# Shorter warm-up, halved first transposes, a halved last product and other places for the last x tiles, in a one-core block kernel with a planned order

## The chip, the cores and the metric

One NeuronCore of a Trainium2 chip runs the whole kernel as one program. The time is the device time of one execution in microseconds (us). The kernel before has a median of 604.91 us over three runs (604.63, 604.91 and 607.84). One further execution was profiled: it took 605.64 us, and its trace spans 603.5 us from the first to the last instruction. The 2.14 us between the two lie around the span.

Engines are called by their short names: PE multiplies matrices (PEld is its weight load), DVE and ACT work on vectors, POOL is GpSimd, and SP issues the DMAs.

## The reference

The input x has 2048 tokens of width 512. What has to be computed, cut to its core:

```python
xn = layernorm(x)                                   # no gain, no bias
q, k, v = split(xn @ wqkv)                          # 32 heads of width 16
phi = lambda t: where(t > 0, t + 1, exp(t)) + 1e-6
kv = einsum("bhsd,bhse->bhde", phi(k), v);  z = phi(k).sum(tokens)
s = (phi(q) @ kv) / (phi(q) . z + 1e-6)  @ wo       # linear attention
g = silu((gelu(xn @ w_gate) * (xn @ w_up)) @ w_down)  # F = 1792
return x + s * g
```

## The kernel before, in words

**Arithmetic.** Every large product is made in float32 accuracy from three single passes: each operand is split into a high part (cast by ACT) and a low part (what is left, subtracted by DVE or POOL), and the passes are high x high, high x low and low x high (`split`, `three`). The FFN products and most of the q and k products are moreover made by a Strassen scheme with seven block products instead of eight, so that DVE, ACT and POOL form sums of blocks and add up results while PE multiplies.

**Stages.** First the tokens are read, normalised (`ln`, L639 to L648), transposed by PE (`transp`, L696, a bank of PSUM named `pt`) and split into `Xh` and `Xl` (`split_x`). The first two pairs of token tiles get plain products for k and q (`plain`, keys "K" and "Q"); later pairs get Strassen products (keys "A"). The sums over tokens for the attention are collected in four banks (`gps`, keys "G"). Then come the two halves of the FFN (keys "F" for gate and up, "E" for down), and the attention's last product (keys "S", tiles `sps`), whose four column chunks are worked in the order 2, 3, 0, 1 (`CHUNKS`). For each of the last chunks `out_tile` multiplies the accumulated and silu'd FFN result (`acc` or a tile `g` read back from DRAM) by the product, adds the matching tile of x (read again, `sxr`) and stores it to `out_yT`.

**The front.** PE begins with idle products of a matrix of ones: `WARM[0]` = 14 of them, each of which is two matmul instructions, in bank 0 (`warm`, L561). Behind the first tile's four transposes stand `WARM[1]` = 3 more. The first tile's four transposes are one piece of work for the planner; its split is made in two halves (each 128x256), which both follow that one piece.

**The end.** The very last product, chunk 1 and n = 3, is 12 matmuls of 512 columns into one bank. Its multiplication, addition and store are made in two column halves, both of which follow the whole product. The last tiles of x are loaded into places shared with `g` and other FFN tiles (`SPOTS`), and a load waits until the tile that was there has been stored.

**What sets the order.** Nothing is issued in the order of the code. Each piece of work is an `Op` with an engine, an assumed cost, and what it depends on. `Plan.order` lays the pieces out with these costs, and then re-deals them: each entry of the table `KEPT` names a stretch of assumed time and a seed, from which pieces there get another due time (`altered`), and the whole order is planned again. The result fixes the order on each engine: PE may take a piece up to 6 us of assumed time (`AHEAD`) out of its listed turn. On the chip each engine then goes through its own list strictly in order and waits where an operand, a bank or a place isn't ready; SP's list of DMAs is in order too. So a piece that waits holds back all that stands behind it on its engine.

Of the kernel before, what the change touches and what calls it, by code (L numbers as in the profile page):

```python
# [16 lines left out]
EPS_LN = 1e-5  # L17
EPS = 1e-6
KEPT = [
    (85, 100, [10000006]),  # L20
    (70, 85, [10000048]),
    (-1, 12, [10000061]),
    (40, 55, [10000175]),
    (135, 200, [10000200]),
    (25, 40, [10000230]),
    (40, 55, [10000342]),
    (85, 100, [10000376]),
    (40, 55, [10000415, 10000462]),
    (500, 560, [10000471]),
    (-1, 12, [10000515]),  # L30
    (500, 560, [10000523, 10000590, 10000640]),
    (115, 135, [10000649]),
    (500, 560, [10000723]),
    (115, 135, [10000785]),
    (500, 560, [10000819, 10000833]),
    (340, 420, [10000924]),
    (115, 135, [10000994]),
    (-1, 12, [10001161, 10001223, 10001300]),
    (270, 340, [10001313, 10001357]),
    (-1, 12, [10001377]),  # L40
    (500, 560, [10001410]),
    (-1, 12, [10001492]),
    (40, 55, [10001818]),
    (-1, 12, [10001854]),
    (500, 560, [10001973]),
    (340, 420, [10002732]),
    (135, 200, [10006848]),
    (85, 100, [10010611]),
    (270, 340, [10010753]),
    (40, 55, [10010839]),  # L50
    (340, 420, [10010858]),
    (500, 560, [10010942, 10011053]),
    (40, 55, [10011765]),
    (135, 200, [10011937]),
    (-1, 12, [1010000092]),
    (340, 420, [1010000637, 1010002072]),
    (25, 40, [1010003933]),
    (500, 560, [1010016325, 1010018040]),
    (70, 85, [1010018047, 1010018667, 1010018893, 1010020523]),
    (55, 70, [1010020607]),  # L60
    (85, 100, [1010021997]),
    (100, 115, [1010030646]),
    (115, 135, [1010032131]),
    (100, 115, [1010033698]),
    (500, 560, [1010034750, 1010034866]),
    (135, 200, [1010038225]),
]

TABLES = {"exp": "exp", "gelu": "gelu", "silu": "silu"}
# [326 lines left out]
def kernel(  # L396
# [66 lines left out]
    def bank(i, name, shape=(P, D)):  # L463
        return tile_in("ps", i, list(shape), F32, name)
# [95 lines left out]
        for _ in range(n):  # L560
            nc.tensor.matmul(o, w, w, start=True, stop=True)  # L561
# [127 lines left out]
    def transp(n, i):  # L689
        t = tokens[n][i]  # L690

        pt = bank(3 + 2 * n + i if 0 < 2 * n + i < 2 * CL else 1, f"pt{t}", (P, KT, P))

        def run(o, a, b):
            for k in range(KT):
                nc.tensor.transpose(o[:, k, :], a[:, k * P:(k + 1) * P], b)  # L696
# [25 lines left out]
    def split_x(n, i):  # L722
        if i == 0 and n == 0:
            for s in range(2):
                split(xrows("h", s, s + 1, [0]), xrows("l", s, s + 1, [0]), pts[0, 0][:, 2 * s:2 * s + 2], 2 * P, "Xa")
# [166 lines left out]
    pe_keys.append(("T", 0, 0))  # L892
    for m, (n, i) in enumerate(tiles):
        plain_keys("K", n, i)
        if m + 1 < len(tiles):
# [381 lines left out]
    def attn(c, M, place):  # L1277
# [29 lines left out]
    def out_tile(c, n, ps):  # L1307
# [9 lines left out]
            parts = 2 if (c, n) == (CHUNKS[-1], KT - 1) else 1  # L1317
            w = NC // parts
            for m in range(parts):
                cs = slice(m * w, (m + 1) * w)  # L1320
                o = columns(g, m, parts)
                if ps.psum:
                    do("DVE", dve(w), lambda o, i: nc.vector.tensor_mul(o, o, i), o, ps[:, cs])
                else:
                    tt("DVE", "mul", o, o, ps[:, cs], w)
# [9 lines left out]
    def sums(c):  # L1335
        return [("S", c, n) for n in range(KT)]

    def between(p, wait, s):
# [89 lines left out]
```

## Time and profile before

| what | value |
|---|---|
| median of the runs shown | 604.91 us |
| the profiled execution's own time | 605.64 us |
| its span | 603.5 us |
| PE busy | 594.2 us (98% of the span) |
| DVE, ACT, POOL busy | 517.0, 347.1 and 243.0 us |
| moved by DMA | 137.09 MB, 227 GB/s over the span |

The profile shows, for each engine, when an instruction ran, how long it was busy, and what ended the idle time ahead of it. PE's matmuls are pipelined: a row says how long they were in flight together, and a 512-column matmul that takes 390 ns follows the last one after some 227 ns. A row of the timeline has the start, the length, the engine, the line of the code, the operation, the tile written and the tiles read, and the number of instructions merged in the row. A row of the windows has the two ends, the length, and then for each engine its busy time and the count of instructions.

### The profile page before, as it was taken

Reading aid. Unit: us, or ns where it says so; the run is one execution under the profiler, and the core shown is the slowest. Engines: PE = TensorE matmul, PEld = TensorE weight load, DVE = VectorE, ACT = ScalarE, POOL = GpSimd, SP = SyncE. Lnnn points to the kernel's source line nnn. Section 1 sums busy time; section 2 is a strip of 40 time slices with the busy share of each in tenths; the row PEclk is TensorE's granted clock in tenths of the full one; section 3 lists DMA queues with packets and bytes.
Section 4 is the critical chain, followed back from the end, with each engine's and each line's share of the span. In section 5 each row is a group of like instructions: output and inputs, shape, how many; then the busy total and the mean of one; then the engine's idle time right before and its main releaser. Section 6 shows DMA issues by size and latency. Waiting matters only on the chain.

```text
span 603.5 us, 7883 instructions
## 1 busy us (share of the span) xinstructions
PE 594.2 (98%) x2636; PEld 483.4 (80%) x2636; DVE 517.0 (86%) x819; ACT 347.1 (58%) x627; POOL 243.0 (40%) x237
## 2 busy tenths in 40 slices
PE   9999999999999999999999999999999999999996
PEld 7887877788878888888888777788888888886885
DVE  6999998787689899999899766668899898987995
ACT  6687888787576655655344566655353444445530
POOL 4456757757535372615053830522222130325000
PEclk9999999999999999999999999999999999999998
DMA  7259954779863344667964999744555665568577
GB/s 243 70 154 273 292 187 137 220 212 352 349 232 129 134 175 174 223 225 270 364 213 153 364 394 351 299 164 153 191 193 191 204 215 190 194 202 295 195 252 259
DMA packets 73384, 137.09 MB, mean 227 GB/s; under 512 B 4352, under 2 KB 43264, under 8 KB 69248
## 3 DMA queue, kind: packets, MB, share of 16 engines
q1 hardware_dynamic: 73344, 136.59, 64.8%
q8 instruction: 21, 0.34, 0.2%
q14 instruction: 19, 0.16, 0.1%
HBM read 85.72 MB, written 50.86 MB: 226 GB/s over the span
## 4 chain that ended last, share of the span: by engine, by line
PE 87%; DVE 6%; DMA 4%; ACT 1%; issue 1%; POOL 0%; DVEq 0%; ACTq 0%; POOLq 0%
PE FX L531 24%; PE FZ L531 12%; PE dX L531 11%; PE gps L531 7%; PE FY L531 6%; PE dZ L531 5%; PE X L531 5%; PE dY L531 3%; PE Z L531 2%; PE k L531 2%; PE q L531 2%; PE sps L531 2%; DMA sxr<-in_A_xT 2%; PE Y L531 1%; DMA pql<-t_d 1%
## 5 line engine op out<-in xcount | busy, mean ns | idle before, releaser
L531 PE MATMUL FX<-Xh,w 128*128 128x512 f32 x448 | 135.2, 391 | 0.0
L531 PEld LDWEIGHTS FX<-Xh,w 128*128 128x128 f32 x448 | 83.9, 188 | 18.3 <-ACT fu L498 0.6
L1194 POOL TENSOR_TENSOR h<-h,g 128x512 f32<-128x512 f32 x28 | 41.3, 1475 | 99.5 <-DVE h L504 95.5
L531 PE MATMUL FZ<-Xh,w 128*128 128x512 f32 x224 | 69.8, 393 | 0.0
L531 PE MATMUL FX<-Xl,w 128*128 128x512 f32 x224 | 68.9, 390 | 0.1
L1154 DVE TENSOR_TENSOR acc<-acc,dX 128x512 f32<-128x512 f32 x76 | 51.8, 681 | 19.4 <-PE dX L531 18.9
L498 ACT CAST hfh<-sums 128x512 fp32r<-128x512 f32 x56 | 34.5, 622 | 48.9 <-DVE sums L504 48.4
L498 ACT COPY fu<-FX 128x512 f32<-128x512 f32 x56 | 32.9, 587 | 42.2 <-PE FX L531 40.6
L504 POOL TENSOR_TENSOR tmp<-raw 128x256 f32<-128x256 f32 x28 | 27.4, 992 | 66.9 <-DVE w L504 35.3
L531 PEld LDWEIGHTS FZ<-Xh,w 128*128 128x128 f32 x224 | 42.0, 188 | 9.9 <-issue 1.0
L531 PEld LDWEIGHTS FX<-Xl,w 128*128 128x128 f32 x224 | 42.0, 188 | 9.2 <-ACT fu L498 0.5
L504 DVE TENSOR_TENSOR hfl<-sums,hfh 128x512 fp32r<-128x512 f32 x56 | 42.5, 764 | 4.2 <-ACT hfh L498 3.3
L531 PE MATMUL dX<-hfl,dh 128*128 128x512 f32 x112 | 43.9, 394 | 1.1 <-DVE acc L1154 0.6
L1007 POOL TENSOR_TENSOR qz<-qz,zq 128x512 f32<-128x512 f32 x16 | 23.4, 1465 | 50.9 <-DMA qz<-q_d 44.5
L531 PE MATMUL dX<-hfh,dl 128*128 128x512 f32 x112 | 43.7, 391 | 0.0
L531 PE MATMUL dX<-hfh,dh 128*128 128x512 f32 x112 | 43.7, 392 | 0.0
L504 POOL TENSOR_TENSOR sums<-draw 128x256 f32<-128x256 f32 x28 | 22.0, 795 | 45.0 <-DMA draw<-in_B_w_down 34.3
L1154 DVE TENSOR_TENSOR acc<-acc,dZ 128x512 f32<-128x512 f32 x52 | 35.5, 683 | 3.9 <-PE dZ L531 3.8
L498 ACT CAST hfh<-h 128x512 fp32r<-128x512 f32 x42 | 26.0, 621 | 15.3 <-POOL h L1194 5.4
L531 PE MATMUL FY<-Xh,w 128*128 128x512 f32 x112 | 34.3, 390 | 0.3 <-ACT FY L498 0.3
L531 PE MATMUL FZ<-Xl,w 128*128 128x512 f32 x112 | 34.3, 390 | 0.0
L504 DVE TENSOR_TENSOR hfl<-h,hfh 128x512 fp32r<-128x512 f32 x42 | 32.8, 781 | 0.0
(197 smaller groups left out, 1490.6 us busy)
## 6 DMA issues: line engine op xcount, KB each, us to landing
w<-w_d SPq DMA_DIRECT2D x17, 1792.0 KB, 7.6
w_d<-w SPq DMA_DIRECT2D x11, 1792.0 KB, 8.0
draw<-in_B_w_down SPq DMA_DIRECT2D x14, 512.0 KB, 6.1
w_d<-we SPq DMA_DIRECT2D x18, 256.0 KB, 3.3
x<-in_A_x SPq DMA_DIRECT2D x16, 256.0 KB, 4.0
q_d<-qp SPq DMA_DIRECT2D x16, 256.0 KB, 2.9
qz<-q_d SPq DMA_DIRECT2D x16, 256.0 KB, 4.5
q<-q_d SPq DMA_DIRECT2D x16, 256.0 KB, 3.3
```

The lines of the kernel that those rows point to most:

```text
L498: do("ACT", act(n, src.psum), lambda o, i: nc.scalar.copy(o, i), dst, src, name=name)
L504: do(eng, c, lambda o, p, q: getattr(e, f"tensor_{op}")(o, p, q), dst, a, b, name=name)
L531: nc.tensor.matmul(o if r is None else o[:, r], a, b, start=first, stop=made == self.passes[r], skip_group_check=self.on or r is not None)
L1007: do("POOL", pool(D), lambda o, z: nc.gpsimd.tensor_mul(o, o, z.unsqueeze(1).to_broadcast([P, KT, P])), rows_of(q), zq, name="u")
L1154: do("DVE", dve(D), lambda o, i: nc.vector.tensor_add(o, o, i), o, ps, name="acc")
L1194: do("POOL", pool(NC), lambda o, i: nc.gpsimd.tensor_mul(o, o, i), h, g, name="h")
```

## The change

It has five parts.

1. **Fewer idle products.** `WARM` goes from 14, 3 to 12, 2, and they use bank 7 instead of bank 0.
2. **The first transposes in two halves.** The first tile's four transposes become two pieces of two, each with half of the bank `pt` as its own resource, so that each half of the split follows its own pair. The remaining idle products stand behind the second pair.
3. **The last product in two column halves.** Chunk 1, n = 3 becomes two sums of 12 matmuls with 256 columns, each in a bank of its own, and its multiplication, addition and store follow half by half.
4. **Places for the last x tiles.** In the last chunk `sxr` goes into `FREED`, the 16 places of the `hfh` and `hfl` tiles, instead of `SPOTS`.
5. **Another deal.** `KEPT` is replaced as a whole, and the assumed cost of a tile's transposes is 0.5 instead of 0.4. This moves instructions on all engines.

The diff, with the table cut to its first line:

```diff
 KEPT = [
-    (85, 100, [10000006]),
+    (-1, 12, [230000004]),
...
-WARM = 14, 3
+WARM = 12, 2
...
-    idle = bank(0, "warm", (P, P))
-    do("PE", 0.427 * 10, warm, idle, ones, key="warm")
+    idle = bank(7, "warm", (P, P))
+    do("PE", 0.427 * 11.5, warm, idle, ones, key="warm")
...
-        pt = bank(3 + 2 * n + i if 0 < 2 * n + i < 2 * CL else 1, f"pt{t}", (P, KT, P))
-        def run(o, a, b):
-            for k in range(KT):
-                nc.tensor.transpose(o[:, k, :], a[:, k * P:(k + 1) * P], b)
-            if n == 0 and i == 0:
-                warm(idle(), ones(), WARM[1])
-        do("PE", 0.4, run, pt, xns[t], ident, key=("T", n, i), name="T", more=(idle,) if n == 0 and i == 0 else ())
+        front = n == 0 and i == 0
+        pt = tile_in("ps", 3 + 2 * n + i if 0 < 2 * n + i < 2 * CL else 1, [P, KT, P], F32, f"pt{t}", 2 if front else 1)
+        for h in range(2 if front else 1):
+            v = pt.part(pt.res[h:h + 1], (slice(None), slice(2 * h, 2 * h + 2))) if front else pt
+            def run(o, a, b, h=h):
+                for k in range(2 if front else KT):
+                    j = 2 * h + k
+                    nc.tensor.transpose(o[:, k, :], a[:, j * P:(j + 1) * P], b)
+                if front and h:
+                    warm(idle(), ones(), WARM[1])
+            do("PE", 0.25 if front else 0.5, run, v, xns[t], ident, key=("T", n, i, h) if front else ("T", n, i), name="T",
+               more=(idle,) if front and h else ())
...
+            if (c, n) == (CHUNKS[-1], KT - 1):
+                halves = []
+                for m in range(2):
+                    cs = slice(m * NC // 2, (m + 1) * NC // 2)
+                    ps = bank(ring("sps", [3, 4, 2, 0, 1]), f"sps{c}{n}{m}", (P, NC // 2))
+                    Sum(ps).add(("S", c, n, m), *three([[v[:, k, rows] for v in M] for k in range(KT)],
+                                                       [[v[:, cs] for v in f] for f in forms_]), name="S", cost=SHORT)
+                    halves.append(ps)
+                out_tile(c, n, halves)
+                continue
...
-            xr = U("g", SPOTS, f"sxr{c}{n}")
+            xr = U(*(("xr", FREED) if c == CHUNKS[-1] else ("g", SPOTS)), f"sxr{c}{n}")
...
+    FREED = [*FHH, *FHL]
```

What this does to the order of the built program, at three places. In each list a row is the line of the code, the operation, what is written and read, and the size; the figures in a name only tell buffers apart.

**First place, the front: SP's DMAs and ACT's casts.** `x` is a tile of tokens, `wk` are the two weight tiles of k (two halves each), `kq` their split. SP before:

```order
L494 DMA x_98<-in_A_x 128x512
L494 DMA wk_119<-in_A_wqkv 128x512 x2
L494 DMA x_124<-in_A_x 128x512
L494 DMA wk_130<-in_A_wqkv 128x512 x2
L494 DMA x_133<-in_A_x 128x512
L494 DMA x_137<-in_A_x 128x512
```

SP in the changed kernel:

```order
L540 DMA x_98<-in_A_x 128x512
L540 DMA x_117<-in_A_x 128x512
L540 DMA wk_123<-in_A_wqkv 128x512 x2
L540 DMA wk_126<-in_A_wqkv 128x512
L540 DMA x_128<-in_A_x 128x512
L540 DMA x_132<-in_A_x 128x512
L540 DMA wk_126<-in_A_wqkv 128x512
```

The second token tile moved from the fourth place to the second, the first weights from second and third to third and fourth, and the last half of the second weights from sixth to eighth. ACT before, from its first weight cast (`pt_156` is the first transposed tile, `pt_196` the second, `xnh` the high part of the tokens):

```order
L498 CAST kq_145<-wk_119 128x512 x2
L498 CAST xnh_166<-xn_152 128x512
L498 CAST Xh_172<-pt_156 128x2x128 x2
L498 CAST kq_145<-wk_130 128x512 x2
L498 CAST xnh_203<-xn_190 128x512
```

ACT in the changed kernel (`pt_159` is the first transposed tile):

```order
L544 CAST kq_154<-wk_123 128x512 x2
L544 CAST Xh_170<-pt_159 128x2x128
L544 CAST kq_154<-wk_126 128x512
L544 CAST xnh_180<-xn_152 128x512
L544 CAST Xh_170<-pt_159 128x2x128
L544 COPY xt_187<-pt_159 128x512
L544 CAST kq_154<-wk_126 128x512
```

The two casts of the first transposed tile no longer stand together: between them stand a cast of the second weights and one of the tokens, and the other half of the second weights comes after both.

**Second place, the first Strassen pair of the tokens: DVE around the split of the last weight form** (`kq` from `wk`, 128x1024). `c` adds a saved result to a bank, `Xl` are low parts of tokens. Before:

```order
L504 TENSOR_TENSOR Xl_183<-T_449,Xh_172 128x4x128 x2
L504 TENSOR_TENSOR Xl_183<-pt_633,Xh_172 128x4x128
L504 TENSOR_TENSOR c_2_664<-u_2_640,Z_575 128x512
L504 TENSOR_TENSOR kq_235<-wk_130,kq_235 128x1024
L504 TENSOR_TENSOR Xl_183<-pt_666,Xh_172 128x2x128
```

In the changed kernel:

```order
L550 TENSOR_TENSOR Xl_178<-T_447,Xh_170 128x4x128
L550 TENSOR_TENSOR Xl_178<-pt_621,Xh_170 128x4x128
L550 TENSOR_TENSOR Xl_178<-T_447,Xh_170 128x4x128
L550 TENSOR_TENSOR kq_297<-wk_126,kq_297 128x1024
L550 TENSOR_TENSOR c_2_668<-u_2_647,Z_601 128x512
```

The split of the weight form now stands ahead of the addition `c` instead of behind it.

**Third place, the end: DVE's last multiplications and additions.** `sps` are the banks of the attention's product, the figure tells them apart. Before:

```order
L504 TENSOR_TENSOR acc_0_4030<-acc_0_4030,sxr_5733 128x512
L504 TENSOR_TENSOR acc_2_3986<-acc_2_3986,sxr_5742 128x512
L1323 TENSOR_TENSOR acc_2_3986<-acc_2_3986,sps_5752 128x512
L504 TENSOR_TENSOR acc_2_3986<-acc_2_3986,sxr_5707 128x512
L1323 TENSOR_TENSOR acc_3_4010<-acc_3_4010,sps_5775 128x512
L504 TENSOR_TENSOR acc_3_4010<-acc_3_4010,sxr_5757 128x512
L1323 TENSOR_TENSOR acc_3_4010<-acc_3_4010,sps_5792 128x256 x2
L504 TENSOR_TENSOR acc_3_4010<-acc_3_4010,sxr_5725 128x256 x2
```

In the changed kernel:

```order
L550 TENSOR_TENSOR acc_0_4027<-acc_0_4027,sxr_5734 128x512
L550 TENSOR_TENSOR acc_2_3983<-acc_2_3983,sxr_5631 128x512
L1386 TENSOR_TENSOR acc_2_3983<-acc_2_3983,sps_5751 128x512
L550 TENSOR_TENSOR acc_2_3983<-acc_2_3983,sxr_5680 128x512
L1386 TENSOR_TENSOR acc_3_4008<-acc_3_4008,sps_5772 128x512
L550 TENSOR_TENSOR acc_3_4008<-acc_3_4008,sxr_5438 128x512
L1384 TENSOR_TENSOR acc_3_4008<-acc_3_4008,sps_5789 128x256
L550 TENSOR_TENSOR acc_3_4008<-acc_3_4008,sxr_5580 128x256
L1384 TENSOR_TENSOR acc_3_4008<-acc_3_4008,sps_5804 128x256
L550 TENSOR_TENSOR acc_3_4008<-acc_3_4008,sxr_5580 128x256
```

The first half is now multiplied and added ahead of the second half's multiplication, and each half has a bank of its own. On SP the last load of an x tile before is `sxr_5757`, with two stores (of `g_5645` and of `acc_0`) ahead of it that stand behind the load of `sxr_5742`; in the changed kernel the last load is `sxr_5734`, and all the remaining stores stand behind it. That load takes the place of `g_5559`, so it waits until that tile is stored.

More of the change, by code (lines that the diff above doesn't have):

```diff
@@ L37 @@
[L37 to L53, printed above, removed]
@@ new lines @@
+    (200, 270, [230000007]),
+    (40, 55, [230000051]),
+    (55, 70, [230000055]),
+    (500, 560, [230000057]),
+    (-1, 12, [230000067]),
+    (270, 340, [230000091]),
+    (500, 560, [230000095]),
+    (115, 135, [230000096]),
+    (500, 560, [230000130]),
+    (115, 135, [230000136]),
+    (70, 85, [230000159]),
+    (270, 340, [230000175]),
+    (500, 560, [230000184]),
+    (-1, 12, [230000189]),
+    (270, 340, [230000192]),
+    (340, 420, [230000237]),
+    (500, 560, [230000265]),
@@ new lines @@
+    (100, 115, [230012249]),
+    (135, 200, [230012251]),
+    (-1, 12, [230012263, 230012268]),
+    (200, 270, [230012291]),
+    (340, 420, [230012323]),
+    (-1, 12, [230012330]),
+    (500, 560, [230012337]),
+    (270, 340, [230012385]),
+    (340, 420, [230012437]),
+    (-1, 12, [230012841]),
+    (115, 135, [230013103]),
+    (500, 560, [230013486]),
+    (270, 340, [230013516]),
+    (85, 100, [230013546]),
+    (40, 55, [230013647]),
+    (500, 560, [230013701]),
+    (12, 25, [230013744]),
@@ L67 @@
+    (115, 135, [230123837]),
+    (-1, 12, [230153839]),
+    (70, 85, [230160428]),
+    (55, 70, [230193669, 230193955, 230215242, 230216530, 230218069]),
+    (500, 560, [230221690]),
+    (55, 70, [230221781]),
+    (12, 25, [230237491]),
+    (500, 560, [230242507]),
 ]
@@ L1335, in sums @@
     def sums(c):
+        if c == CHUNKS[-1]:
+            return [("S", c, n) for n in range(KT - 1)] + [("S", c, KT - 1, m) for m in range(2)]
         return [("S", c, n) for n in range(KT)]
```

89 lines of the change are left out of this document (56 added, 33 removed).

## The prediction

> **What bounds the kernel now.** The page comes first: how busy is PE, and what is the chain made of that ends last.
>
> ```profile
> span 603.5 us, 7883 instructions
> PE 594.2 (98%) x2636; PEld 483.4 (80%) x2636; DVE 517.0 (86%) x819; ACT 347.1 (58%) x627; POOL 243.0 (40%) x237
> PE 87%; DVE 6%; DMA 4%; ACT 1%; issue 1%; POOL 0%; DVEq 0%; ACTq 0%; POOLq 0%
> ```
>
> PE is the bound: 594.2 of 603.5 us. The change takes no product away that matters, so it can only win what PE loses, 9.3 us in all, and the end that follows PE. Where these lie is read from the windows (ends, length, PE busy), cut at PE's first and last matmul and around its worst stretch.
>
> ```profile
> 0.00:1.12 1.12, 0.00 (x1) 1.00 0.00 0
> 1.12:540.00 538.88, 537.35 (x2394) 1.00 0.65 225
> 540.00:560.00 20.00, 18.81 (x78) 1.00 0.74 260
> 560.00:598.10 38.10, 38.01 (x168) 1.00 0.73 255
> 598.10:603.50 5.40, 0.00 (x0) 0.69 0.42 153
> ```
>
> 5.40 us lie behind the last matmul, 1.19 us between 540 and 560, 1.53 us in the 539 us before that, and 1.12 us ahead of the first. The middle hides a little more: a matmul of 512 columns counts as busy for 0.39 us though the next follows after 0.227 (48 of them in the 11.04 us of the row at 586.96 below). So there are three places to price: the front, the deal in the middle, the end. I work against the profiled execution's own 605.64 us, which is 0.73 above the median shown (604.91), and take that off at the end.
>
> **The front.** The timeline shows PE's idle products, the first transposes, and the first products for k, and what they stand on.
>
> ```profile
> 3.50 0.69 DVE L639 BATCH_NORM_STATS2 st<-x 128x6 f32<-128x512 f32 x1 [2.43 <-DMA x<-in_A_x]
> 1.25 0.89 SPq L494 DMA_DIRECT2D wk<-in_A_wqkv  x2
> 2.65 0.91 SPq L494 DMA_DIRECT2D wk<-in_A_wqkv  x2
> DMA to landing us min/median/max: 3.0/4.7/5.4
> 4.26 0.62 ACT L498 CAST kq<-wk 128x512 fp32r<-128x512 f32 x1 [1.88 <-DMA wk<-in_A_wqkv]
> 5.78 0.62 ACT L498 CAST kq<-wk 128x512 fp32r<-128x512 f32 x1 [0.90 <-DMA wk<-in_A_wqkv]
> 6.31 0.61 ACT L498 CAST xnh<-xn 128x512 fp32r<-128x512 f32 x1
> 7.41 0.65 ACT L498 CAST Xh<-pt 128x256 fp32r<-128x256 f32 x2 [0.49 <-PE pt L696]
> 7.99 1.23 ACT L498 CAST kq<-wk 128x512 fp32r<-128x512 f32 x2
> 6.48 1.28 POOL L504 TENSOR_TENSOR kq<-wk,kq 128x512 fp32r<-128x512 f32 x1 [1.24 <-ACT kq L498]
> 5.28 0.55 DVE L648 TENSOR_SCALAR xn<-x,mv,rstd 128x512 f32<-128x512 f32 x1 [0.67 <-POOL rstd L644]
> 1.12 5.82 PE L561 MATMUL warm<-ones 128*128 128x128 f32 x28 [1.12 <-DVE neg_half L552]
> L561 PE MATMUL warm<-ones x34: 275/421/582, 1.1 to 7.8; 128*128 128x128 f32 x34
> 6.77 0.60 PE L696 MATMUL pt<-ident,xn 128*128 128x128 f32 x4
> 7.21 0.83 PE L561 MATMUL warm<-ones 128*128 128x128 f32 x6
> 8.14 1.17 PE L531 MATMUL k<-kq,Xh 128*128 128x512 f32 x4
> 12.71 0.70 POOL L644 TENSOR_TENSOR rstd<-ve,neg_half 128x2 f32<-128x2 f32 x1 [1.66 <-DVE ve L642]
> 14.44 0.66 PE L696 MATMUL pt<-ident,xn 128*128 128x128 f32 x4
> 15.77 2.11 PE L531 MATMUL k<-kq,Xh 128*128 128x512 f32 x8
> ```
>
> *Idle products.* The normalised tile is ready at 5.28 + 0.55 = 5.83, but the transposes begin at 6.77: they wait for the idle products, not for data. The six in the row at 7.21 follow each other by (0.83 - 0.28) / 5 = 0.11 us (275 ns is the shortest time that one of them is in flight, by the row of the tile `warm`). Two products fewer are four instructions, 4 x 0.11 = 0.44 us: transposes at 6.3. The third product of the second batch was in nobody's way once ACT's casts (to 8.06) release the first k product at 8.14.
>
> *The first half's split* could then start near 6.3 + 2 x 0.11 + 0.2 = 6.7. But ACT's list decides. Before, tiles land in the order x, wk, wk, x, wk, wk: the weights at about 4.25, 5.75, 8.0 and 8.5 (issues 1.25, 1.7, 2.65, 3.1 with the landing times of their row; the third from the median). Now x comes second, so the weights are third, fourth, fifth and eighth: about 5.75, 6.5 (between its neighbours), 8.0 and, three tiles behind 8.0 at 0.65 each, 9.9. The first k product in the new list needs the low weights from POOL: cast 5.78 to 6.40, subtraction 1.28 as in its row, so 7.8. Four products are possible there; the fifth needs the second half of `Xh`, and this cast now stands behind a weight cast that waits for 8.0, and behind `xnh`: 8.0 + 0.62 + 0.55 + 0.35 = 9.5. Before, the fifth ran at 8.14 + 4 x 0.23 = 9.1. So the first product gains 0.3, the fifth loses 0.4, and the last weights, 9.9 + 0.62 for the cast (behind a copy, so 10.7) + 1.3 to 1.75 on POOL, come at 12.0 to 12.5.
>
> What ends the front is the transposes of the second pair at 14.44 and the dense run from 15.77. They hang on POOL's `rstd`, which stands behind that last weight split: 12.5 + 0.7 + 0.55 = 13.8, early enough. I take **0** for the front, with bounds of -0.5 (all that the idle products free) and +0.8 (the cast of the last weights ended at 7.99 + 1.23 = 9.2 and now at 10.7; half of the 1.5 us if other products fill the rest).
>
> A page of the Trainium skill speaks against fewer idle products: TensorE: Matmul & The Clock Gate, Part 1, has PE at half rate until it has been busy for a free-running window of about 3.4 us, whose phase differs from run to run. This trace bears out a gate: the 28 of the first row take 5.82 us, twice the 0.11 us each of the six later ones.
>
> **The deal in the middle.** One wait can be read off the new order. The second list of the change is about it; these are its rows.
>
> ```profile
> 52.25 0.68 DVE L504 TENSOR_TENSOR c<-u,Z 128x512 f32<-128x512 f32 x1
> 52.85 1.32 DVE L504 TENSOR_TENSOR kq<-wk,kq 128x1024 fp32r<-128x1024 f32 x1
> 53.35 0.63 PE L531 MATMUL Z<-kq,Xh 128*128 128x512 f32 x2
> 54.22 0.72 PE L531 MATMUL Z<-kq,Xh 128*128 128x512 f32 x2 [0.24 <-DVE kq L504]
> ...
> 553.57 0.62 ACT L498 CAST pql<-pql 128x512 fp32r<-128x512 f32 x1 [1.92 <-DMA pql<-t_d]
> ```
>
> The third product of Z was due at 53.35 + 2 x 0.227 = 53.80 and came at 54.22; the restart costs 0.1 more (0.72 against 0.63). With `kq` ahead of `c`, its split starts 0.60 earlier (52.25 instead of 52.85), so the wait of 0.42 goes: **-0.5**, bounds -0.6 and 0 (if ACT's cast for it is late too).
>
> What comes next there is `c`, 1.3 later, which no product of that stretch reads. All other waits of the middle are re-dealt without my being able to say which way: the largest group, 1.19 us idle between 540 and 560, hangs on the load of a chunk of q (`pql`), whose place on SP and whose distance from PE's last use of the place to PE's first use of the chunk (33 matmuls instead of 34) are nearly as before. I take 0 for them, with bounds of -1.5 (half of the 1.19 and 1.53 us, somewhat more with restarts) and +1.5 (as much the other way).
>
> **The end.** The timeline of PE's last four products and DVE's last pieces, and the landing of this stretch's x loads:
>
> ```profile
> 586.96 11.04 PE L531 MATMUL sps<-pql,M 128*128 128x512 f32 x48
> 595.79 0.69 DVE L504 TENSOR_TENSOR acc<-acc,sxr 128x512 f32<-128x512 f32 x1 [2.65 <-DMA sxr<-in_A_xT]
> 596.40 0.68 DVE L1323 TENSOR_TENSOR acc<-acc,sps 128x512 f32<-128x512 f32 x1
> 599.05 0.74 DVE L1323 TENSOR_TENSOR acc<-acc,sps 128x256 f32<-128x256 f32 x2
> 599.72 0.75 DVE L504 TENSOR_TENSOR acc<-acc,sxr 128x256 f32<-128x256 f32 x2
> ...
> DMA to landing us min/median/max: 5.2/5.5/6.5
> ```
>
> PE is done at 586.96 + 11.04 = 598.00. DVE, which lost 2.65 us on an x tile, starts the last product's halves only at 599.05 and ends at 600.47, 2.47 us behind PE; the last store and the program's end take 3.03 more (603.5).
>
> *With x in time*, the first half is multiplied when its 12 short matmuls are done, some 1.36 us ahead of PE's end, and DVE is free for the second half: two short pieces of 0.37 (two are 0.74 and 0.75 in the rows) and a little for the hops, 0.8 us from PE's end to the last addition, against 2.47. That is -1.6. The cover is the x tiles: behind the addition of the last load, `sxr_5734`, stand five pieces of 0.65 and the first half's two of 0.36 that must be through at 598.0, so it must start by 598.0 - 0.7 - 6 x 0.65 = 593.4. The load waits for the store of `g_5559`, whose last addition stands 24 pieces ahead of DVE's end, some 15 us, at about 583; with 5 us for the store (as for a load, by the nearest row) and 5.5 for the load it lands near 593.5. I take **-1.5**, with bounds of -1.6 and -0.5 (landing 1.1 later).
>
> *Short matmuls.* 24 of 256 columns replace 12 of 512. No row has this shape; two rows bound it:
>
> ```profile
> 157.68 3.73 PE L1034 MATMUL pkv<-GT,wvo 128*128 128x128 f32 x32
> L531 PEld LDWEIGHTS FX<-Xh,w 128*128 128x128 f32 x448 | 83.9, 188 | 18.3 <-ACT fu L498 0.6
> ```
>
> 32 matmuls with a weight load each follow by (3.73 - 0.28) / 31 = 0.111 us; 24 of these are 2.67 us against 12 x 0.227 = 2.72. If each had to wait for a whole load of 0.188, 24 would be 4.51, or +1.8. I take **0**, by the first row, since loads there do overlap.
>
> The Trainium skill (TensorE: Matmul & The Clock Gate, LDWEIGHTS (loading the stationary operand)) gives a load as columns / 1.2 GHz, an estimate of 107 ns for 128. By it the 24 are 2.6 us, and the sum stays; the 188 ns of the row are a load's own duration, and the 0.111 agrees with the page.
>
> **The sum.** Front 0, middle -0.5, end -1.5, short matmuls 0: 605.64 - 2.0 = 603.6 for an execution like the profiled one, and 0.73 less, 602.9, beside the median.
>
> **The rivals.**
>
> *The front gives back what it took* (the loads re-ordered: weights later). For it: the fifth product, 0.4 late, and the 1.5 us of the last weights. Against: `rstd` has 0.6 us of room. With +0.8: 603.7.
>
> *The clock gate opens later*, since the front does less. For it: the half rate of the first 5 us. Against: the four instructions taken away came after it had opened, and data holds the k products until 7.8 anyway. Were PE at half rate for a further window, the first eight products or so would take 0.23 longer each: +1.8, 604.7. The page named above would allow this.
>
> *Loads of weights bound the short matmuls*: +1.8, 604.7. Against: 0.111 us in the row of the 32.
>
> *Slower: the last x load lands late.* DVE takes its list in order, and from this load's addition to its end are 6 x 0.65 + 4 x 0.36 = 5.4 us. In this trace an x tile made DVE wait until 595.79, and the load in question waits for a store first. Landing at 596.5, 3.1 behind its time, it ends DVE at 601.9 instead of 600.47: +1.4 where -1.5 was, so 605.8. It decides from 595.6 on: 595.6 + 5.4 - 600.5 = +0.5, which eats the middle's 0.5.
>
> *More: the new deal also takes waits of 540 to 560 and others*: -1.5, 601.4.
>
> **How the numbers follow.** Forecast (601.9 to 604.0) 0.53; front given back 0.13; gate 0.03; weight loads 0.06; late x load 0.10; more waits gone 0.15. The range leaves out half of the last two: 601.0 to 605.3. A measurement of this kernel can hardly tell less than 0.5% from no change, here 3.0 us, so the bounds are 601.9 and 607.9. Faster: the case of more waits gone and a little of the forecast's edge, 0.18. Slower by so much needs the late load and a bad deal together, 0.04. Within: 0.78.
>
> **What would show each step.** Transposes at 6.3 and the first k product at 7.8, then a gap on PE near 9; the dense run from 15 to 16.5. No wait for `kq` near 53. At the end the gap from PE's last matmul to the last addition near 0.8, no wait of DVE for `sxr` beyond 593.5, and the last two `sps` groups at 0.11 per matmul. I am wrong if PE's idle time between 16 and 590 us changes by more than 1.5 us, if the short matmuls follow by over 0.13, or if DVE waits for the last x load.

## The result and the profile after

The changed kernel is slower: a median of 609.73 us over seven executions (608.23 to 611.96), beside 604.84 us for the kernel before (603.66 to 607.84). The ratio is 1.0083, with a 95% interval of 1.0064 to 1.0101. The prediction was 602.9 us with a range up to 605.3, and a slowdown of more than 0.5% had a chance of 0.04 in it. It was wrong. The profiled execution of after took 611.06 us, 5.42 more than that of before (605.64), and I account for these 5.42. It ran at a mean granted clock of 0.997, the execution with the median time at 1.000; what that costs is said at B.

The page of after, first the span, PE's share and the chain that ended last:

```profile
span 608.8 us, 7893 instructions
PE 595.5 (98%) x2642; PEld 484.2 (80%) x2642; DVE 516.3 (85%) x819; ACT 346.5 (57%) x627; POOL 242.0 (40%) x237
PE 82%; DVE 8%; DMA 6%; ACT 2%; issue 1%; POOL 1%; SPq 0%; ACTq 0%; DVEq 0%; POOLq 0%
```

PE is busy for about as long as before. What has grown is what the chain holds beside PE: 18% instead of 13%, with DMA and DVE in it. The windows of after behind its first matmul, cut as those of before were (ends, length, PE busy and count, then PEld, DVE, ACT, POOL, the granted clock, DMA share, GB/s):

```profile
1.12:540.00 538.88, 531.82 (x2358) 433.05 (x2359) 454.92 (x720) 320.88 (x584) 230.57 (x222) 1.00 0.65 224
540.00:560.00 20.00, 19.45 (x86) 15.46 (x84) 18.44 (x30) 8.50 (x16) 7.23 (x8) 1.00 0.64 212
560.00:605.10 45.10, 44.20 (x201) 35.67 (x201) 41.95 (x67) 16.78 (x29) 3.72 (x3) 1.00 0.79 267
605.10:608.80 3.70, 0.00 (x1) 0.00 (x0) 0.84 (x2) 0.00 (x0) 0.00 (x0) 1.00 0.25 85
```

Up to 540 us PE now idles for 7.06 us (538.88 - 531.82) where it idled for 1.53. The end behind PE is 3.70 us long where it was 5.40. So the end came out shorter by about what was forecast, and the middle ate it three times over. Busy time hides part of a gap, so I also took from the trace how far each matmul starts behind the one ahead of it, beyond 0.2267 us for 512 columns, 0.12 for 256 and 0.11 for 128 (less where it starts early), and added that up by stretch:

| stretch, us | before | after | difference |
|---|---|---|---|
| 0 to 20 | 3.84 | 4.52 | +0.68 |
| 20 to 380 | 6.97 | 7.67 | +0.70 |
| 380 to 400 | 0.71 | 2.48 | +1.77 |
| 420 to 460 | 0 | 4.33 | +4.33 |
| 540 to 580 | 2.82 | 1.74 | -1.08 |
| 580 to PE's end | 0.15 | 1.32 | +1.17 |
| end behind PE | 5.47 | 3.74 | -1.73 |

That is +5.84. The first row isn't time lost: an idle product counts as work in this measure, and the six idle matmuls that are gone are 0.66 us of it, while the dense run of products starts at 15.77 us in both kernels. The 24 short matmuls are 0.16 us more work than the 12 that they replace. Both together leave +5.34, and the two spans (603.47 and 608.84 us) differ by 5.37; the last 0.05 of the 5.42 lie outside them. The 0.70 us between 20 and 380 came with the new order and weren't taken apart (the run in the old order below has 6.99 there). Three places carry it. I call them A, B and C.

**A, at 391 us.** PE waits for a bank that ACT's copy `dY<-dX` reads. PE in before and in after, then ACT in before and in after, then DVE in after:

```profile
391.80 0.50 PE L531 MATMUL dX<-hfl,dh 128*128 128x512 f32 x1 [0.43 <-DVE hfl L504]
```
```profile
394.06 0.50 PE L577 MATMUL dX<-hfh,dh 128*128 128x512 f32 x1 [2.19 <-ACT dY L544]
```
```profile
389.82 0.57 ACT L498 COPY dY<-dX 128x512 f32<-128x512 f32 x1
```
```profile
392.41 0.63 ACT L1170 ACTIVATE g<-g 128x512 f32<-128x512 f32 x1 [2.26 <-DVE g L550]
...
393.46 0.55 ACT L544 COPY dY<-dX 128x512 f32<-128x512 f32 x1
```
```profile
386.58 1.76 DVE L550 TENSOR_TENSOR sums<-h,h 128x512 f32<-128x512 f32 x1 [1.47 <-POOL h L1245]
...
391.70 0.68 DVE L550 TENSOR_TENSOR g<-fu,FZ 128x512 f32<-128x512 f32 x1
```

A gelu now stands ahead of the copy on ACT; in before it came behind it (at 391.18). It waits 2.26 us for DVE's multiplication at 391.70, which is late because DVE's work ahead of it runs slowly: 1.76 us in the row of 386.58, for a shape that takes 0.69 elsewhere, while POOL is at work beside it. DVE was as slow there in before (1.67 us for an addition at 386.58), but the copy did not hang on it.

**B, at 435 us.** PE's bank for `dZ` comes free with DVE's addition `acc<-acc,dX`. In the new order DVE's reduction of `qz` stands ahead of that addition. (`qz` is a tile of q, read back from DRAM, multiplied by z on POOL and summed on DVE: the attention's denominators, which are needed only later.) PE, DVE, POOL and SP in after:

```profile
434.79 0.39 PE L577 MATMUL dX<-hfh,dl 128*128 128x512 f32 x1
437.64 0.50 PE L577 MATMUL dZ<-hfh,dh 128*128 128x512 f32 x1 [2.47 <-DVE acc L1205]
```
```profile
436.30 0.69 DVE L1060 TENSOR_REDUCE rall<-qz 128x32 f32<-128x512 f32 x1 [3.97 <-POOL qz L1058]
436.91 0.68 DVE L1205 TENSOR_TENSOR acc<-acc,dX 128x512 f32<-128x512 f32 x1
```
```profile
435.01 1.26 POOL L1058 TENSOR_TENSOR qz<-qz,zq 128x512 f32<-128x512 f32 x1 [16.15 <-DMA qz<-q_d]
```
```profile
415.49 11.88 SPq L540 DMA_DIRECT2D w<-w_d  x2
427.59 0.32 SPq L540 DMA_DIRECT2D qz<-q_d  x1
```

Read it from the last row up: the load of `qz` is issued at 427.59, right behind a load of weights `w`, and lands some 7.4 us later; POOL multiplies, DVE reduces, DVE adds, PE goes on. In before the load was no faster (issued at 425.69, multiplied from 432.63 on), but DVE had its additions ahead of the reduction, and nobody who was needed stood behind it. DVE and POOL in before:

```profile
429.98 0.69 DVE L1154 TENSOR_TENSOR acc<-acc,dX 128x512 f32<-128x512 f32 x1 [0.16 <-PE dX L531]
...
432.70 0.69 DVE L1154 TENSOR_TENSOR acc<-acc,dX 128x512 f32<-128x512 f32 x1 [1.43 <-PE dX L531]
...
434.59 0.68 DVE L1009 TENSOR_REDUCE rall<-qz 128x32 f32<-128x512 f32 x1
```
```profile
432.63 1.29 POOL L1007 TENSOR_TENSOR qz<-qz,zq 128x512 f32<-128x512 f32 x1 [16.27 <-DMA qz<-q_d]
```

B costs more than its wait: the start at 437.64 is 2.85 behind the one at 434.79, 2.62 too late, and a further 1.7 follows, most of it because PE then runs at half rate for 3.4 us. The windows of after around A and B, cut at the recorded changes of the clock and at whole steps of 3.41 us from them (the granted clock is the third number from the right):

```profile
390.37:393.78 3.41, 1.50 (x7) 0.92 (x5) 3.38 (x6) 1.37 (x3) 2.00 (x2) 1.00 0.08 34
...
434.74:438.15 3.41, 0.94 (x4) 0.48 (x4) 1.81 (x5) 0.43 (x1) 1.26 (x1) 1.00 0.19 55
438.15:441.56 3.41, 3.41 (x9) 2.68 (x9) 2.26 (x4) 0.08 (x1) 1.07 (x1) 0.50 0.23 67
```

Nine matmuls fit into the last window where fifteen would at 0.227: 6 x 0.227 = 1.4 us.

**C, at 588 us.** DVE waits for a tile `g`, and PE for a bank that DVE's multiplication behind it frees. PE, DVE and SP in after, then SP in before:

```profile
589.24 4.83 PE L577 MATMUL sps<-pqh,M 128*128 128x512 f32 x20 [0.87 <-DVE g L1386]
```
```profile
588.50 1.46 DVE L1386 TENSOR_TENSOR g<-g,sps 128x512 f32<-128x512 f32 x2 [1.27 <-DMA g<-g_d]
```
```profile
580.38 0.33 SPq L540 DMA_DIRECT2D g<-g_d  x1
581.65 0.81 SPq L540 DMA_DIRECT2D sxr<-in_A_xT  x2
582.54 0.87 SPq L540 DMA_DIRECT2D g<-g_d  x2
```
```profile
571.66 1.22 SPq L494 DMA_DIRECT2D g<-g_d  x2
```

The two loads of x at 581.65 (one of them for the last chunk, with its new place) now stand ahead of the two loads of `g` at 582.54, the first of which is the tile `g31` that DVE waits for. In before `g31` is the second load of the row at 571.66, ahead of both loads of x, and DVE does not wait for it.

**The front and the end** of this execution went nearly as forecast. PE's front in after, then PE's last row and DVE's last two:

```profile
6.00 0.66 PE L746 MATMUL pt<-ident,xn 128*128 128x128 f32 x4 [0.26 <-DVE ve L688]
...
7.95 1.04 PE L577 MATMUL k<-kq,Xh 128*128 128x512 f32 x2 [0.85 <-POOL kq L550]
...
15.77 1.89 PE L577 MATMUL k<-kq,Xh 128*128 128x512 f32 x7
```
```profile
597.77 7.34 PE L577 MATMUL sps<-pql,M 128*128 128x512 f32 x43
```
```profile
605.14 0.42 DVE L1384 TENSOR_TENSOR acc<-acc,sps 128x256 f32<-128x256 f32 x1 [0.56 <-PE sps L577]
605.60 0.42 DVE L550 TENSOR_TENSOR acc<-acc,sxr 128x256 f32<-128x256 f32 x1
```

The dense run starts at 15.77, to the hundredth as before. PE ends at 597.77 + 7.34 = 605.11 and DVE at 606.02, 0.91 behind it instead of 2.47, without a wait for x.

### The profile page after: what moved, and what is told of

Read it like the earlier page. It is cut to its first block, busy times and chain, and to the rows that moved or that the text cites. A ratio compares the mean times of both kernels' runs of the same rounds, so it can differ in the third digit from the quotient of the medians.

```text
span 608.8 us, 7893 instructions
## 1 busy us (share of the span) xinstructions
PE 595.5 (98%) x2642; PEld 484.2 (80%) x2642; DVE 516.3 (85%) x819; ACT 346.5 (57%) x627; POOL 242.0 (40%) x237
## 4 chain that ended last, share of the span: by engine, by line
PE 82%; DVE 8%; DMA 6%; ACT 2%; issue 1%; POOL 1%; SPq 0%; ACTq 0%; DVEq 0%; POOLq 0%
PE FX L577 22%; PE FZ L577 11%; PE dX L577 10%; PE gps L577 6%; PE FY L577 6%; PE dZ L577 5%; PE X L577 5%; PE sps L577 4%; PE dY L577 3%; PE Z L577 2%; DVE hfl L550 2%; PE k L577 2%; PE q L577 2%; DVE sums L550 2%; DMA g<-g_d 2%; DVE acc L1205 1%
## 5 line engine op out<-in xcount | busy, mean ns | idle before, releaser
L550 POOL TENSOR_TENSOR tmp<-raw 128x256 f32<-128x256 f32 x28 | 25.6, 927 | 51.5 <-DVE w L550 32.5
L550 DVE TENSOR_TENSOR hfl<-sums,hfh 128x512 fp32r<-128x512 f32 x56 | 40.4, 731 | 3.2 <-ACT hfh L544 2.3
L550 DVE TENSOR_TENSOR sums<-h,h 128x512 f32<-128x512 f32 x28 | 24.9, 891 | 9.1 <-POOL h L1245 9.1
```

Source lines behind the costliest of these rows:

```text
L550: do(eng, c, lambda o, p, q: getattr(e, f"tensor_{op}")(o, p, q), dst, a, b, name=name)
```

## The experiments

**Theory:** the code edits do what the prediction says (front 0, end about -1.5), and the new order costs the rest at A, B and C, B most. **Rivals:** an edit in the code brings the waits about (loads of x that come earlier, banks); or the waits are exchangeable, so that the next one steps in when one is removed. Ratios are to the kernel before on the same chip, with 95% intervals.

### Code and order apart

`e1_old_order` has after's code, but each engine gets before's order; `e2_new_order` the other way round. The order is written out as a list of the pieces' numbers (first halves of the split pieces are put beside the second):

```diff
+LISTED = [0, 2, 5, 1, 4, ...]
-    for o in plan.order([part for key in pe_keys for part in subs.get(key, [key])]):
+    order = [plan.ops[n] for n in LISTED]
+    for o in order:
         o.fn()
```

> The changed code (14 idle products and 24 short ones fewer or more as in the change, transposes and last product in halves, last x tiles in places of their own), but every engine's instructions in the order of before, written out as a list. Theory (the new order costs it all): the front is 0, the end gains 1.6, the waits of after at 391, 435 and 588 us are gone, so 604.8 - 1.6 = 603.2, and PE's first half of the products reads like before. Rival (one of the edits in the code does it, by new waits or by loads of x that come earlier and take the queue): 608 to 610, and PE waits at the same three places.

> The code of before in the order of after (only what its own dependencies forbid is put later: some loads of x at the end). Theory: the waits at 391 and 435 us come back here, the end stays 5.4 us long, so 604.8 + 2 + 4 + 0.5 = 611.3 or a little more, slower than after. Rival (the edits): 605, as before.

Measured: e1 604.14 us beside 605.26 (ratio 0.9989, 0.9976 to 1.0002); e2 611.16 (1.0090, 1.0057 to 1.0124). After's code without its order costs nothing and perhaps wins a microsecond; before's code in after's order is as slow as after, and its trace has A and B again (2.01 us lost between 380 and 400, 4.95 between 420 and 460), but not C (0.16 beyond 580). So by these traces A and B are the order's alone, and C needs the edits and the order together. e1's end, PE and DVE:

```profile
585.88 11.19 PE L761 MATMUL sps<-pql,M 128*128 128x512 f32 x60
```
```profile
597.44 0.76 DVE L734 TENSOR_TENSOR acc<-acc,sxr 128x256 f32<-128x256 f32 x2
```

DVE ends at 598.20, 1.13 behind PE's 597.07: 1.3 us less than before in the trace, 1.1 between the medians. I had expected 1.6.

### Each wait by itself

`e3_gelu_behind` and `e4_den_behind` move a few pieces behind others in after's order (the numbers are those of the pieces; 2578 is the gelu, 2504 the copy, 2357 the reduction, 2693 the addition to `acc` of `dZ`):

```diff
+    order = plan.order([...])
+    for a, b in ((2577, 2481), (2578, 2504)):                                  # e3
+    for a, b in ((2357, 2693), (2360, 2357), (2358, 2759), (2359, 2358)):      # e4
+        order.remove(plan.ops[a])
+        order.insert(order.index(plan.ops[b]) + 1, plan.ops[a])
```

> After, with ACT's gelu of the row at 392.41 put behind the two copies at 392.95 and 393.46, and the multiplication on DVE that it waits for put behind the low part hfl. Theory (this gelu holds PE, because it stands ahead of the copy that frees the bank): the wait of 2.19 us at 391.5 shrinks to 0.6 or less; 609.7 - 1.6 = 608.1. Rival (PE would have waited for hfl, which POOL's sums slow down, just as long): at most 0.5 is won, 609.2.

> After, with DVE's reduction of qz of the row at 436.30 (and its two small followers, and the load that takes qz's place) put behind the next additions to acc. Theory (the reduction waits for a load, and PE's bank waits behind it): the wait of 2.47 us at 435 goes, and with it the half rate of the 3 us after it: 609.7 - 2.7 = 607.0 where no half rate had followed, 4.1 less where it had; median near 606.5. Rival (PE next waits for something else, the later load of q above all): 609 or more.

Measured: e3 608.47 us (1.0059, 1.0038 to 1.0080), e4 606.63 (1.0028, 1.0010 to 1.0046). Both are near what was expected (608.1; 606.5). e4's interval lies below that of after (1.0064 to 1.0101); e3's, from five executions, overlaps it, so what undoing A is worth rests on its trace more than on the medians. In e3 the copies run at 389.89 and 390.52, and PE passes A with 0.2 us lost:

```profile
390.52 0.57 ACT L544 COPY dY<-dX 128x512 f32<-128x512 f32 x1
392.59 0.64 ACT L1170 ACTIVATE g<-g 128x512 f32<-128x512 f32 x1 [1.50 <-DVE g L550]
```

In e4 DVE adds at 433.73 and 434.41 and reduces at 435.05 without a wait, and PE loses nothing between 400 and 540:

```profile
433.73 0.69 DVE L1205 TENSOR_TENSOR acc<-acc,dX 128x512 f32<-128x512 f32 x1 [1.43 <-PE dX L577]
434.41 0.69 DVE L1205 TENSOR_TENSOR acc<-acc,dZ 128x512 f32<-128x512 f32 x1
435.05 0.69 DVE L1060 TENSOR_REDUCE rall<-qz 128x32 f32<-128x512 f32 x1
```

In these two traces the waits aren't exchangeable: each goes without another growing. With A gone, 4.50 us stay between 420 and 460 and 1.26 beyond 580 (e3); with B gone, 2.54 stay between 380 and 400 and 1.18 beyond 580 (e4).

### All three

`e5_three_fixed` adds (3497, 3473) to the moves of e3 and e4: the load of `g31` goes up in the order. On SP's queue, which the compiler arranges, it came to stand behind `g32` and ahead of `sxr10` and `sxr33`, not ahead of all three.

> After with three moves: ACT's gelu and its multiplication as in e3, DVE's reduction of qz as in e4, and the load of g31 on SP's queue put ahead of the loads g32, sxr10 and sxr33, behind which it stood when DVE waited for it at 588.5 us. Theory (these three places are the whole difference): the waits at 391, 435 and 588 us are gone together, 609.7 - 1.7 - 3.1 - 1.0 = 603.9, with a granted clock of 0.999 to 1.0, and about the time of the run in the old order (604.1). Rival (waits that move on, as when one is taken away the next comes): 606 or more.

Measured: 603.53 us beside 605.13, ratio 0.9975 (0.9963 to 0.9987). This is the fastest version here, faster than before by 1.6 us, and the only one whose interval lies below 1. Expected were 603.9. Between 380 and 400 PE loses 0.76 us, from 400 to 540 nothing, beyond 580 0.20. C was not undone by itself: its share of about 1 us rests on the traces.

### B put into before

`e6_before_den` moves the reduction in before to where after has it, ahead of the addition of 429.98; `e12_den_later` puts it one addition further back, ahead of the one of 432.70.

```diff
+    for a, b in ((2355, 2734), (2356, 2355)):      # e6; e12: (2355, 2746), (2356, 2355)
```

> Before with one move: DVE's reduction of qz (in before the row at 434.59) put ahead of the addition acc<-acc,dX of the row at 429.98, as the new order has it; nothing else. Theory: DVE stands until the load of qz has landed and POOL has multiplied it (433.9 us), PE waits 2.5 us for a bank, and some executions lose 1.5 to 2 more by half rate: 605.3 + 2.5 to 4.3, near 608.5. Rival (the wait is hidden by other products of PE): within 1 us of before.

> As the run with the reduction ahead in before, but one place further back: behind the addition of 429.98 and the low part, ahead of the addition acc<-acc,dX of 432.70. Theory (the price is how long DVE stands there while PE's bank waits): the addition ends at 435.2 instead of 433.4, so PE waits about 1.3 us instead of 2.6, and without the half rate behind it, since the wait is short: 606.5. Rival (any wait of PE for this load brings the half rate too, or the wait is as long): 608 or more.

Measured: e6 608.57 us (1.0062, 1.0036 to 1.0088), as expected; e12 605.39 beside 604.81 (1.0010, 0.9999 to 1.0021), where I had expected 606.5. First e6, PE and DVE:

```profile
434.73 0.80 PE L531 MATMUL dZ<-hfh,dh 128*128 128x512 f32 x1 [2.41 <-DVE acc L1154]
```
```profile
433.40 0.69 DVE L1009 TENSOR_REDUCE rall<-qz 128x32 f32<-128x512 f32 x1 [3.91 <-POOL qz L1007]
```

then e12, DVE and PE:

```profile
434.67 0.69 DVE L1009 TENSOR_REDUCE rall<-qz 128x32 f32<-128x512 f32 x1 [2.72 <-POOL qz L1007]
```
```profile
436.01 0.50 PE L531 MATMUL dX<-hfh,dh 128*128 128x512 f32 x1
```

DVE stands at the reduction until 433.40 in e6 and until 434.67 in e12. But in e12 the addition it holds up frees a bank that PE takes only at 436.01, and PE comes 0.1 us late. One addition further back in DVE's list is the difference between 0.2 us and 4.2 (lost between 420 and 460). My 1.3 for e12 assumed that PE needs the bank of the next addition at once; it needs it only near 435.9. The windows of e6 show the half rate again, behind a window with 1.14 us of PE:

```profile
431.18:434.59 3.41, 1.14 (x6) 0.60 (x4) 1.19 (x2) 0.59 (x1) 1.26 (x1) 1.00 0.36 139
434.59:438.00 3.41, 3.27 (x8) 2.60 (x9) 2.67 (x6) 0.00 (x0) 0.22 (x1) 0.50 0.32 77
```

### Why the reduction stands there

The first part of this document says that the plan fixes the order on each engine. For SP it doesn't: `ENGINES`, the engines whose order is written out, leaves SP out, and the compiler arranges SP's queue. The numbers in the tiles' names follow the plan; the number ahead of a row is its place on SP. After, and below it `e7_sp_as_planned`:

```
184 L540 DMA w20_4163<-w_d_88 128x3584
185 L540 DMA w21_4276<-w_d_88 128x3584
186 L540 DMA qz7_4270<-q_d_83 128x512
```
```
183 L540 DMA w20_4163<-w_d_88 128x3584
184 L540 DMA qz6_4169<-q_d_83 128x512
185 L540 DMA qz7_4270<-q_d_83 128x512
186 L540 DMA w21_4276<-w_d_88 128x3584
```

In the new plan qz7 (4270) comes ahead of w21 (4276), a load seven times as large, and the reduction is placed by that; in the program it comes behind. In before plan and program agree: `w21_4271`, then `qz7_4280`, and the reduction stands late. e7 puts SP under the plan too:

```diff
-ENGINES = {..., mybir.EngineType.Pool}
+ENGINES = {..., mybir.EngineType.Pool, mybir.EngineType.SP}
```

> After, with SP's queue too in the order of the plan (SP added to the engines whose order is written out; before and after leave it to the compiler). In the plan the load qz7 stands ahead of the load of w21, in after's program behind it. Theory (the reduction stands so early because the plan has its load ahead of w21, and the program has not): the load lands some 10 us earlier, the wait of 2.47 us at 435 us is gone without a change on DVE, the waits at 391 and 588 stay: 606.6, as in e4. Rival (the load itself is slow, whatever its place): 609 or more.

Measured: 605.51 us beside 605.13 (1.0004, 0.9989 to 1.0019): 4.5 us less than after, each taken beside its own before, though no move was made on DVE. SP, POOL and DVE of e7:

```profile
415.02 12.05 SPq L540 DMA_DIRECT2D qz<-q_d  x2
427.17 0.38 SPq L540 DMA_DIRECT2D w<-w_d  x1
```
```profile
429.52 1.29 POOL L1058 TENSOR_TENSOR qz<-qz,zq 128x512 f32<-128x512 f32 x1 [5.14 <-DMA qz<-q_d]
```
```profile
431.36 0.68 DVE L1060 TENSOR_REDUCE rall<-qz 128x32 f32<-128x512 f32 x1
```

The reduction no longer waits. (e7 exchanges neighbours at nine places of SP's queue, not at this one alone; but A and C stay, with 1.98 and 1.02 us lost, and nothing is lost any more between 420 and 460.) The load isn't issued 10 us earlier, as I had expected, but at about the same time (the second of the two in the row of 415.02 goes out at its end, near 426.8); POOL has it some 2.7 us later instead of 7.4, with w21 behind it and not ahead.

`e10_planned_fixed` adds the moves for A and C to e7:

> After with SP's queue in the order of the plan (as in e7) and the two other moves of e5 (ACT's gelu with its multiplication; the load of g31 ahead of g32, sxr10 and sxr33); DVE's reduction stays where the new order has it. Theory (once the load stands where the plan has it, the place of the reduction costs nothing): 605.5 of e7 less 1.6 and 0.9 for the two waits it still had, 603.0, like e5 (603.5) or a little less, and faster than before by 1.6 to 2. Rival (the reduction ahead still holds something up): 604.5 or more.

Measured: 604.23 us beside 604.95 (0.9992, 0.9982 to 1.0003), a miss by 1.2 us. A is down to 0.70, but at C there are now two waits. PE and SP of e10:

```profile
582.39 1.20 PE L577 MATMUL sps<-pqh,M 128*128 128x512 f32 x4 [0.47 <-DVE g L1386]
...
584.20 4.85 PE L577 MATMUL sps<-pqh,M 128*128 128x512 f32 x20 [0.61 <-DVE g L1386]
```
```profile
577.26 0.80 SPq L540 DMA_DIRECT2D g<-g_d  x2
```

Here `g31` really stands ahead of `g32`. SP stands still until 577.26, when `g31` is issued, and `g32` behind it follows some 3 us later than in e4 (574.60). In e5, which has them the other way round, PE does not wait. The profiled execution is the slowest of the eleven (606.22 us), so how much of these two waits stands in the median stays open, and the intervals of e10 and e5 (0.9963 to 0.9987) overlap a little. A load put early can hold up the queue behind it just as a waiting piece does on an engine.

### The parts of the change by themselves

In before's order: `e8_places_only` is before's code with only the new places for x, `e9_halves_only` is e1 with the old places for x, and `e11_front_only` is before's code with only the front changed.

```diff
-            xr = U("g", SPOTS, f"sxr{c}{n}")
+            xr = U(*(("xr", FREED) if c == CHUNKS[-1] else ("g", SPOTS)), f"sxr{c}{n}")    # e8; e9 undoes it
```

> Before's code in before's order; only the last chunk's four x tiles get places of their own (their loads move up on SP). Theory (DVE's wait of 2.65 us for an x tile goes; the last product stays whole, so from PE's end come its two multiplications and two additions, 4 x 0.36 + 0.2 = 1.6 us where 2.47 were): 0.8 less than before, 604.5. Rival (the loads come earlier and hold up those of g): PE waits near 580 us, and the time is before's or more.

> The run in the old order with the last x tiles back in the places of g: of the end only the two column halves of the last product are left (the front's edits stay). Theory (halves are worth nothing while DVE is late): DVE still waits some 2.6 us for an x tile near 595 us and ends as in before, about 2.4 us behind PE's last product; 605.1, within 0.4 of before. Rival (halves alone bring the end forward): 604.2 or less.

> Before's code in before's order; only the front is changed (14 idle products instead of 17, the first transposes in two halves with splits of their own). Theory (the front is hidden: the dense run of products still starts where the second pair's transposes allow): 0, so 605.1, within 0.5; the dense run at 15.5 to 16. Rivals: PE half a microsecond earlier, 604.6; or the clock gate opens later, up to 606.9.

Measured: e8 604.85 us beside 605.13 (0.9997, 0.9985 to 1.0010), e9 604.95 beside 604.81 (1.0003, 0.9993 to 1.0013), e11 604.78 beside 604.81 (0.9998, 0.9989 to 1.0007). None can be told from before. The front is 0, as forecast: the interval of e11 rules out a gain or a loss of more than 0.7 us. Of the end neither half of the edit shows a gain by itself; in e9 DVE still waits for x, 0.95 us for the tile at 597.22, with 2.0 us of its list from there on. One reason lies in before's own executions. In the profiled one DVE waited 2.65 us for an x tile near the end; in e11 and e12, whose code of the end is before's, no wait for x from 592 us on is longer than 0.36, and DVE ends 1.46 us behind PE instead of 2.47. e8 ends 1.46 behind PE too. So the places can help only in executions in which x is late, and how many these are isn't known.

## Why the prediction was wrong, step by step

*The front, 0 (bounds -0.5 to +0.8): right.* Transposes at 6.00 (forecast 6.3), the first k product at 7.95 (7.8), the fifth at 9.41 (9.5), the dense run at 15.77. What the idle products freed was lost again before the transposes of the second pair, on which the dense run hangs, as the working had it. The later weights aren't needed for that: in e11, whose loads keep before's order, the first k product comes at 7.43 and the dense run still at 15.74, because DVE waits 1.09 us for another tile of x (until 13.21) ahead of the `xn` of these transposes.

*The middle, -0.5 for the wait for `kq`, and "I take 0 for them", with bounds of -1.5 and +1.5, for all other waits: here it failed.* The wait for `kq` did go. The rest was not 0 but about +6.9 in the table, from 20 us on (0.70 + 1.77 + 4.33 - 1.08 + 1.17; the `kq` wait is in it). The mechanism behind the bound was wrong, not only its size: I bounded the re-dealt waits by the waits that before had, half of 1.19 and 1.53 us. But a new order makes waits where before had none, and what one of them costs is set by how late the thing is that it waits for. The working compares the lists at places where before had waited. Nowhere does it ask which pieces that wait for a DMA had moved ahead of pieces that free PE's banks. The reduction of `qz` had, and before's own rows gave the price: `qz` multiplied at 432.63 + 1.29 = 433.92, an addition that ran at 429.98 put behind it, hence up to some 4 us for DVE. e6 shows that this one move costs before 3.4 us between the medians.

*The end, -1.5: right in how it works, too large for the median.* The two profiled executions differ by 1.7. With before's order (e1) the medians differ by 1.1, and the interval (-1.45 to +0.1 us) just leaves the forecast out: the end is worth about 1 us in the time rather than 1.5. The working took 1.5 off the profiled execution, whose x was late by 2.65 us, and then off the median too, as if x were late in every execution; against e11 and e12, where DVE ends 1.46 us behind PE, the 0.91 of after is only 0.55 less. That x comes in time with the new places was right.

*Short matmuls, 0: right.* PE's last row holds 43 matmuls in 7.34 us: (7.34 - 0.28) - 19 x 0.227 leaves 2.75 us for the 23 steps between the 24 short ones, 0.12 each; the mark I had set was 0.13.

*The rivals.* The one for "slower" (the last x load late) did not occur. "The clock gate opens later" was the right device at the wrong place: in the profiled execution the gate closed in the middle, behind a wait of PE. The working had it only at the front.

Against the order of before and the order mended at three places, the forecast of 602.9 us is 1.2 and 0.6 short (e1 604.14, e5 603.53).

## What to carry to other kernels

When an order is dealt anew, don't bound its new waits by the old ones: go through each in-order list for pieces that wait for a DMA and have moved ahead of pieces that free what the bound engine needs, and price each by when that DMA landed in the trace of before and when the freed thing is needed. A plan is as good as its agreement with the program, so look whether the queue of loads stands as the plan assumed it. A wait of 2.5 us on PE may cost half as much again in clock.

## What the hardware did that I had not expected

PE's clock fell to half in the middle of the kernel behind a wait of 2.4 to 2.6 us (2.41 in e6, 2.47 in after, 2.63 in e3): for 3.41 us, after a step of 3.41 us in which PE had been busy for 1.14 (e6), 0.94 (after) or 0.78 us (e3). A step with 1.50 us of PE (A, in after's profile) did not do it. When all fourteen profiles are cut into steps of 3.41 us from the recorded changes of the clock, no step with 1.50 us of PE or more is followed by half rate, and every step with less that has another behind it in the trace is; the highest of these, 1.27 us, lies at the end of before. The seven executions of after have a mean granted clock of 1.000 (608.2 to 609.7 us), 0.997 (609.2 and 611.1) and 0.994 (611.7 and 612.0), and one half-rate step takes 0.003 off the mean (3.41 x 0.5 of 608 us), so the same waits close the gate in some executions only. (An idle end lowers the mean too, but less here: in before's profile the clock fell 2.15 us behind PE's last product, and of after's end of 3.74 us that would leave 1.6 at half rate, 0.001 of the mean.) e4, where A is the one long wait left, has five executions of 604.9 to 606.1 us at 0.999 or 1.000 and five of 607.1 to 609.4 at 0.997; e5, without A and B, has none below 0.999. That A closes the gate in those five is likely, but no profile here shows it. The Trainium skill (TensorE: Matmul & The Clock Gate, HAM oscillation — how this bites in real kernels) gives the rule "no PE-idle gaps >~3.4µs". The half-rate step of 3.41 us agrees with the free-running window that the page describes in Part 1; the limit doesn't: here idle gaps of 2.4 us are enough when they fill most of one window.

DVE's additions and subtractions of 512 columns that read two tiles in SBUF take 0.69 us alone, and between 386 and 392 us mostly 1.1 to 1.8 beside POOL (the row of 386.58), in before too; the multiplication that reads a bank takes 0.68 beside POOL (the row of 391.70). It is this that makes the pieces of A late in both kernels. That the new order pays for it, and before hardly, is the place of the gelu on ACT: e3 puts it back and PE loses 0.2 us there.
